# One half of a weight cast from GpSimd to VectorE, and other column groups for the last output tile

## The chip, the cores and the metric

The kernel runs on one core of one Trainium2 chip. Times are device microseconds of whole executions. A profile covers one execution, the span from its first to its last instruction, which is some 1.8 us shorter than the time.

Three marks in the profile are used throughout. H is the start of the first w_in matmul, T the start of the first matmul of the last output tile, and E the end of the span (to a hundredth, from the trace). The span is then the sum of H, the way T - H, and the tail E - T. (Differences are of the rounded marks, so good to 0.01.) The front is the start-up together with the cast of the second weight piece (below), which runs beside the first matmuls.

In the profile's lines PE is TensorE, PEld its weight loads, DVE VectorE, ACT ScalarE, POOL GpSimd and SP SyncE; a q marks an engine's queue, which waits and issues transfers; L385 is a line of the kernel. A timeline's line gives start, length, engine, line, operation, what is written <- what is read, shape and count, and in brackets the idle time before and what ended it.

## The reference

Linear attention, then a feed-forward layer, with the attention's heads side by side as the model dimension:

```python
def _attn_ref(q, k, v):            # 8 batches, 8 heads, 576 rows, 64 columns
    q_s = softmax(q, axis=-1)      # (written out with max, exp, sum)
    k_s = softmax(k, axis=2)       # over the rows
    kv = np.einsum('bhsd,bhse->bhde', k_s, v)
    return np.einsum('bhsd,bhde->bhse', q_s, kv)

def _moe_ref(x, w_in, w_out):      # x 4608 x 512, w_in 512 x 2048, w_out 2048 x 512
    h = x @ w_in
    g = 0.5 * h * (1.0 + erf(h / sqrt(2)))
    return g @ w_out
```

## The kernel before

Inputs and weights come as fp32 and are cast to bf16 on the core. The weights come in pieces, each cast when it has landed; w_in has five, of 256, 256, 512, 512 and 512 columns. The cast of the second is one of the two places that change. (`cast_wi` as it was; `r` is 2 for the second piece, and 4 for the later ones.)

```python
    def cast_wi(i, w, eng):
        n = wi_cols[i]
        r = n // 128
        o = wi_bf[:, :, wi_off[i]:wi_off[i] + n].rearrange("p d (c m) -> p d c m", c=r)
        w = w[:, :, 0:n].rearrange("p d (m c) -> p d c m", c=r)
        if eng == "p":
            for h in range(2):
                nc.gpsimd.tensor_copy(out=o[:, 2 * h:2 * h + 2], in_=w[:, 2 * h:2 * h + 2])
        else:
            for c in range(NDM):
                nc.vector.tensor_copy(out=o[:, c], in_=w[:, c])
    # ...
    for dm in range(NDM):
        cast_wi_dm(0, wi[0], dm, nc.gpsimd)      # first piece, GpSimd, four casts
    # ...
    x_evac(0, 2, "s")                            # xT copies, ScalarE and VectorE
    x_evac(0, 3)
    cast_wi(1, wi[1], "p")                       # second piece, GpSimd, two casts
    table(AF.Gelu)
    # ...
    h_phase(0, {                                 # first w_in matmuls of batch 0
        0: [lambda: cast_wi(2, wi[2], "v")],     # third piece, VectorE, four casts
        # ...
    }, groups={0: 2, 4: 4, 8: 4}, banks={...})
```

`h_phase` begins with column tiles 0 and 1 together (eight matmuls, first piece), then tile 2 and tile 3 (second piece), each over the four contraction blocks `dm`. GpSimd's first cast of the second piece gives blocks 0 and 1, its second gives 2 and 3.

The other place is the end. The last output tile is computed in two column groups, so that most of it is on its way out when the last group finishes:

```python
    def y_last():
        j = J - 1
        for i, (c0, n) in enumerate(((0, 384), (384, 128))):
            ps = psum_y.tile([128, DM], FP32, tag="y")
            for t in range(NDF):
                nc.tensor.matmul(
                    ps[:, 0:n], st[B]["g"][:, t, j * 128:(j + 1) * 128],
                    wo_bf[:, t, c0:c0 + n], start=(t == 0), stop=(t == NDF - 1),
                )
            y_sb = moe_sb.tile([128, DM], FP32, tag="y_sb")
            nc.vector.tensor_copy(out=y_sb[:, 0:n], in_=ps[:, 0:n])
            for b2 in range(2):
                r0 = (2 * j + b2) * S + M
                eng = nc.scalar if b2 else nc.sync
                eng.dma_start(
                    out=out[r0:r0 + R, c0:c0 + n], in_=y_sb[b2 * R:(b2 + 1) * R, 0:n]
                )
```

The softmax here doesn't subtract the row's maximum and nothing guards it: scores larger than these inputs give would overflow.

## Time and profile before

| | before |
|---|---|
| time, median of 3 runs | 279.69 us (279.55 to 280.07) |
| span of the profiled run, E | 277.94 us |
| TensorE busy | 271.6 us, 98% |
| H, T | 14.06, 270.88 us |
| way T - H, tail E - T | 256.82, 7.06 us |

The prediction below shows the page's busy table, the waits and the chain of waits (columns: start, length, what; each piece is what released the next). Only the two copies of the last tile are shown here, by form, from 270 us on. The columns are line, engine, operation, tiles, shape and count, then busy time and mean ns of one, then idle time before.

```profile
L385 DVE COPY y_sb<-ps 128x384 f32<-128x384 f32 x1 | 0.6, 558 | 1.9 <-PE ps L380 1.9
L385 DVE COPY y_sb<-ps 128x128 f32<-128x128 f32 x1 | 0.3, 290 | 0.3 <-PE ps L380 0.3
```

The longer copy has 256 columns more and takes 268 ns more.

### The profile page before, as it was taken

Reading aid. Unit: us, or ns where it says so; the run is one execution under the profiler, and the core shown is the slowest. Engines: PE = TensorE matmul, PEld = TensorE weight load, DVE = VectorE, ACT = ScalarE, POOL = GpSimd, SP = SyncE. Lnnn points to the kernel's source line nnn. Section 1 sums busy time; section 2 is a strip of 40 time slices with the busy share of each in tenths; the row PEclk is TensorE's granted clock in tenths of the full one; section 3 lists DMA queues with packets and bytes.
Section 4 is the critical chain, followed back from the end, with each engine's and each line's share of the span. In section 5 each row is a group of like instructions: output and inputs, shape, how many; then the busy total and the mean of one; then the engine's idle time right before and its main releaser. Section 6 shows DMA issues by size and latency. Waiting matters only on the chain.

```text
span 277.9 us, 4563 instructions
## 1 busy us (share of the span) xinstructions
PE 271.6 (98%) x1918; PEld 126.1 (45%) x1918; DVE 100.6 (36%) x153; ACT 157.9 (57%) x246; POOL 33.4 (12%) x27
## 2 busy tenths in 40 slices
PE   7799999999999999999999999999999999999995
PEld 3444454444444444444444444444444444444443
DVE  2876574319743540093008400651015200130012
ACT  4867675789377816791569246943683363136400
POOL 1530041002020220014000500050005000000000
PEclk9999999999999999999999999999999999999999
DMA  7999999963992148712981199117502500220033
GB/s 249 396 400 429 398 400 407 398 251 100 297 341 60 68 107 255 294 38 87 247 346 41 43 234 389 46 49 189 115 0 75 151 2 0 75 78 0 0 78 77
DMA packets 44981, 50.10 MB, mean 180 GB/s; under 512 B 20385, under 2 KB 29857, under 8 KB 44705
## 3 DMA queue, kind: packets, MB, share of 16 engines
q1 hardware_dynamic: 44560, 49.39, 53.2%
q10 hardware_dynamic: 400, 0.43, 0.6%
q8 instruction: 15, 0.25, 0.4%
q14 instruction: 6, 0.04, 0.1%
HBM read 36.70 MB, written 9.44 MB: 166 GB/s over the span
## 4 chain that ended last, share of the span: by engine, by line
PE 93%; DMA 4%; POOL 1%; ACTq 0%; SPq 0%; issue 0%; DVE 0%
PE ps L355 44%; PE ps L327 43%; DMA w<-in_moe_w_in_dram 2%; DMA touch<-in_moe_w_in_dram 2%; PE kv L199 2%; PE ps L294 1%; PE ps L380 1%; PE pair L327 1%; POOL wi_bf L428 1%; POOL wi_bf L439 1%; PE ps L299 0%; PE tp L255 0%; ACTq L482 0%; PE ps L255 0%; ACTq L101 0%; SPq L103 0%
## 5 line engine op out<-in xcount | busy, mean ns | idle before, releaser
L327 PE MATMUL ps<-xT,wi_bf 128*128 128x512 bf16 x568 | 125.1, 379 | 0.1
L355 PE MATMUL ps<-wo_bf,g 128*128 128x512 bf16 x560 | 124.2, 379 | 0.0
L333 ACT ACTIVATE g<-ps 128x512 bf16<-128x512 f32 x142 | 83.6, 598 | 67.0 <-PE ps L327 66.9
L327 PEld LDWEIGHTS <-wi_bf 128*128 128x128 bf16 x576 | 56.1, 98 | 68.2 <-POOL wi_bf L428 0.5
L355 PEld LDWEIGHTS <-g 128*128 128x128 bf16 x560 | 53.9, 98 | 64.3 <-issue 0.4
L363 DVE COPY y_sb<-ps 128x512 f32<-128x512 f32 x33 | 22.6, 686 | 81.0 <-PE ps L355 80.6
L238 POOL TENSOR_TENSOR e<-e,recq 128x2048 bf16<-128x2048 bf16 (+1 forms) x9 | 25.7, 2856 | 175.3 <-DVE recq L237 147.2
L162 DVE CAST v_aug<-f 128x576 bf16<-128x576 f32 x24 | 16.4, 745 | 48.8 <-DMA f<-in_v_dram 48.8
L236 DVE TENSOR_REDUCE qsum<-e 128x16 f32<-128x1024 bf16 (+1 forms) x13 | 21.1, 1620 | 13.9 <-ACT e L145 13.9
L320 ACT CAST xT<-ps 128x512 bf16<-128x512 f32 x18 | 9.9, 588 | 28.1 <-PE ps L294 18.1
L145 ACT ACTIVATE e<-f 128x512 bf16<-128x512 f32 (+1 forms) x42 | 20.5, 556 | 3.2 <-DMA f<-in_q_dram 3.0
L150 ACT ACTIVATE ek<-f 128x2304 bf16<-128x2304 f32 (+1 forms) x10 | 17.2, 1728 | 0.6 <-DMA f<-in_k_dram 0.6
L318 DVE CAST xT<-ps 128x512 bf16<-128x512 f32 x17 | 11.0, 685 | 17.0 <-PE ps L294 14.1
L79 ACT ACT_TABLE_LOAD x9 | 11.5, 1283 | 2.8 <-issue 2.6
L472 PE MATMUL ps<-zeros 128*128 128x512 f32 x14 | 8.6, 779 | 1.4 <-DVE zeros L497 1.4
L145 ACT ACT_TABLE_LOAD x7 | 9.0, 1283 | 0.1
L431 DVE CAST wi_bf<-w 128x512 bf16<-128x512 f32 x12 | 7.4, 648 | 2.2 <-DMA w<-in_moe_w_in_dram 2.0
L199 PEld LDWEIGHTS <-ek 64*64 64x64 bf16 x576 | 6.4, 105 | 2.7 <-issue 0.6
L199 PE MATMUL kv<-v_aug,ek 64*64 64x65 bf16 x576 | 6.8, 193 | 0.5 <-POOL v_aug L162 0.5
L238 DVE TENSOR_TENSOR e<-e,recq 128x1024 bf16<-128x1024 bf16 x4 | 6.3, 1565 | 0.1
L472 PEld LDWEIGHTS ps<-zeros 128*128 128x128 f32 x14 | 3.5, 258 | 5.7 <-issue 4.3
L294 PE MATMUL ps<-qT,kvc 64*64 64x512 bf16 x62 | 5.4, 389 | 0.4 <-DVE kvc L218 0.4
(37 smaller groups left out, 49.9 us busy)
## 6 DMA issues: line engine op xcount, KB each, us to landing
out_dram<-y_sb SPq DMA_DIRECT2D x32, 256.0 KB, 2.4
f<-in_k_dram SPq DMA_DIRECT2D x6, 1152.0 KB, 10.2
f<-in_v_dram SPq DMA_DIRECT2D x6, 1152.0 KB, 11.8
f<-in_q_dram SPq DMA_DIRECT2D x6, 1024.0 KB, 7.2
w<-in_moe_w_in_dram SPq DMA_DIRECT2D x6, 512.0 KB, 8.6
f<-in_v_dram SPq DMA_DIRECT2D x8, 288.0 KB, 6.6
f<-in_q_dram SPq DMA_DIRECT2D x4, 512.0 KB, 8.8
w<-in_moe_w_out_dram SPq DMA_DIRECT2D x2, 1024.0 KB, 11.6
```

The costliest lines, as they stand in the source:

```text
L79: nc.scalar.activation(out=scr[:, 1:2], in_=scr[:, 0:1], func=func)
L145: nc.scalar.activation(out=dst[:, i], in_=src[:, u], func=AF.Exp)
L150: nc.scalar.activation(out=ek[b % 2][:, i:i + n], in_=st[b]["kf"][:, i:i + n].rearrange("p x (n d) -> p x n d", n=NS), func=AF.Exp,)
L162: eng.tensor_copy(out=o, in_=i)
L199: nc.tensor.matmul(st[b]["kv"][hp][c, 0:D + 1], ek[b % 2][pr, hp, n, :], v_aug[b % 2][pr, hp, n, 0:D + 1], start=(n == 0), stop=(n == NS - 1),
L236: nc.vector.reduce_sum(out=qsum, in_=eq[:, :, hs, :], axis=AX.X)
L238: eng.tensor_tensor(out=eq[:, :, hs, :], in0=eq[:, :, hs, :], in1=recq.unsqueeze(3).to_broadcast([128, J, w, D]), op=ALU.mult,)
L327: nc.tensor.matmul(ps, wi_bf[:, dm, t * 128:(t + 1) * 128], st[c]["xT"][:, dm, :], start=(dm == 0), stop=(dm == NDM - 1),)
L333: nc.scalar.activation(out=st[c]["g"][:, t, :], in_=ps, func=AF.Gelu)
L355: nc.tensor.matmul(ps, st[c]["g"][:, t, j * 128:(j + 1) * 128], wo_bf[:, t, :], start=(t == 0), stop=(t == NDF - 1),)
L363: nc.vector.tensor_copy(out=y_sb, in_=ps)
L472: nc.tensor.matmul(ps, z[:, 0:128], z, start=True, stop=True)
```

## The change

Its intent: the second half of the second piece should be ready sooner, since VectorE is idle beside GpSimd there; and the first group of the last tile should leave sooner.

```diff
-        for i, (c0, n) in enumerate(((0, 384), (384, 128))):
+        for i, (c0, n) in enumerate(((0, 320), (320, 192))):
...
-        if eng == "p":
-            for h in range(2):
-                nc.gpsimd.tensor_copy(out=o[:, 2 * h:2 * h + 2], in_=w[:, 2 * h:2 * h + 2])
+        if eng == "pv":
+
+            nc.gpsimd.tensor_copy(out=o[:, 0:2], in_=w[:, 0:2])
+            nc.vector.tensor_copy(out=o[:, 2:4], in_=w[:, 2:4])
...
-    cast_wi(1, wi[1], "p")
+    cast_wi(1, wi[1], "pv")
```

## The prediction

> **What bounds the kernel now.** I read the page's busy table and its 40 slices first, then TensorE's waits, then the chain of waits in order of time, and last the timelines of the two places that the change touches.
>
> ```profile
> PE 271.6 (98%) x1918; PEld 126.1 (45%) x1918; DVE 100.6 (36%) x153; ACT 157.9 (57%) x246; POOL 33.4 (12%) x27
> ...
> PEclk9999999999999999999999999999999999999999
> ```
>
> TensorE is busy for 271.6 of 277.9 us at the full clock; no other engine reaches 60%. Work moved between GpSimd (12%) and VectorE (36%) is therefore worth only what TensorE waits for it.
>
> ```profile
> PE ps L472 <- DVE zeros L497: 1.4, 1, 1.4
> PE ps L255 <- DVE e L238: 0.5, 1, 0.5
> PE kv L199 <- POOL v_aug L162: 0.5, 1, 0.5
> PE ps L294 <- DVE kvc L218: 0.4, 1, 0.4
> ```
>
> These are all the waits of the matmul row: 2.8 us, all in the first 14 us, and none of them is for the cast that the change splits. That wait shows only in the chain of waits, because the modelled end of the matmul before it covers the gap:
>
> ```profile
> 13.27 0.05 issue
> 13.32 1.48 POOL wi_bf L439 x4
> 14.80 1.59 POOL wi_bf L428 x2
> 16.40 0.05 issue
> 16.45 5.35 PE ps L327 x24
> ...
> 271.04 3.51 PE ps L380 x32
> 274.55 0.02 issue
> 274.57 0.29 DVE y_sb L385
> ```
>
> Between 16.45 and 274.55 us the chain is TensorE alone, back to back. So there are just two places at which this change can act: the moment before 16.45, where the chain arrives from GpSimd's two casts (L428), and the end, after the last matmul. Everything between is passed on unchanged unless a new gap opens.
>
> At the first place the timelines of weight loads, GpSimd and VectorE read:
>
> ```profile
> 14.05 1.84 PEld L327 LDWEIGHTS <-wi_bf 128*128 128x128 bf16 x10 [0.23 <-issue]
> 16.44 0.55 PEld L327 LDWEIGHTS <-wi_bf 128*128 128x128 bf16 x4 [0.55 <-POOL wi_bf L428]
> ...
> 14.75 0.64 POOL L428 CAST wi_bf<-w 128x512 bf16<-128x512 f32 x1
> 15.34 1.05 POOL L428 CAST wi_bf<-w 128x512 bf16<-128x512 f32 x1
> ...
> 13.58 1.32 DVE L318 CAST xT<-ps 128x512 bf16<-128x512 f32 x2
> 15.25 2.15 DVE L431 CAST wi_bf<-w 128x512 bf16<-128x512 f32 x3 [0.36 <-DMA w<-in_moe_w_in_dram]
> 18.53 0.62 DVE L431 CAST wi_bf<-w 128x512 bf16<-128x512 f32 x1 [1.13 <-DMA w<-in_moe_w_in_dram]
> ```
>
> Ten weight loads run before the gap: eight for the first two column tiles (first w_in piece) and two for tile 2, that is, contraction blocks 0 and 1, which GpSimd's first cast wrote. The eleventh needs block 2, from the second cast, and waits. VectorE is empty from the end of its two xT copies (13.58 + 1.32 = 14.90) to 15.25, where it waits for the next piece's transfer.
>
> **What the Trainium skill says.** "SBUF — State Buffer", section "Who interferes with whom": GpSimd and a VectorE copy or cast in a two-port mode lock a shared port pair against each other, and the one that issued first makes the other wait. The trace agrees that they disturb each other, though not with a clean lock: GpSimd's cast took 0.64 us beside VectorE's copies from PSUM and 1.05 us beside the L431 casts, and of those the one that began at 15.89 took 0.97 where the median is 0.62. "TensorE: Matmul & The Clock Gate", section "Back-to-back issue gap", gives N/2.4 + 2.5 ns warm: 216 ns for 512 columns, 162 for 384, 136 for 320, 82.5 for 192, 56 for 128. The trace agrees: 10.36 us for 48 matmuls of 512 columns in the chain is 216 ns, and 16 x (162 + 56) = 3.49 us against the chain's 3.51. "DMA: Bandwidth & Descriptors", section "Specifications", puts the smallest transfer at line rate at 512 B; the last piece's rows of 128 columns already are 512 B, and of 192 columns 768 B, so no threshold is crossed.
>
> **The change, part by part.**
>
> Part one, the cast. Removed: one GpSimd cast of 128x512. Added: one VectorE cast of the same size. The gap is worth less than it looks. Weight loads sat idle 0.55 us, but matmuls had one in hand. The first of the ten starts at 14.06 and they follow at 0.216, so an eleventh without a wait starts at 14.06 + 10 x 0.216 = 16.22. It started at 16.45. Hence at most 0.23 us.
>
> Does the new order free all of it? VectorE is free at 14.90. Unhindered, the new cast takes some 0.62 us (like L431's 128x512 casts) and ends at 15.5. If GpSimd's cast, begun at 14.75, holds it up, add the 0.35 us that L431 lost in such an overlap: 15.9. Block 2 is wanted by a weight load at about 16.0, so even then it is there. GpSimd's remaining cast covers blocks 0 and 1, wanted by the weight load at 15.58: undisturbed it ends at 14.75 + 0.64 = 15.39, in time; if instead it is the one slowed to 1.05 us, it ends at 15.80, and the matmul due at 15.79 starts at about 15.95, which gives back 0.16 us. GpSimd starts 0.15 us ahead, so I hold the first more likely (two in three): 0.23 x 2/3 + 0.07 x 1/3 = 0.18 us gained.
>
> Is it given back behind? VectorE's three casts of the third piece start up to 0.65 us later, from 15.5 to 15.9, but lose the collision that cost 0.35; they end at 17.4 to 17.8, before the fourth waits for its transfer until 18.53. From there VectorE's times stand. TensorE, 0.23 earlier, meets these: block 3 of the third piece, cast by 18.53 + 0.62 = 19.15, wanted at about 20.1; the transfer-bound v casts of batch 1, which GpSimd ends at 42.84, against matmuls that would start at 43.41 - 0.23 = 43.18. Both hold, so the gain goes through to the end. The weight buffer of the second piece is also freed up to 0.5 us sooner, which lets a w_out load be queued earlier, but the DMA slices there read 9 and the rate is some 400 GB/s: it is queued behind others and lands at the same time.
>
> Part two, the last tile. Matmuls: 16 x (136 + 82.5) = 3.50 us against 3.49, no change in the end of TensorE. The two L385 copies took 558 ns (384 columns) and 290 ns (128 columns): 268 ns for 256 columns, 1.05 ns each, so 491 ns for 320 and 357 ns for 192. The last copy lies bare after the last matmul, and so costs 357 - 290 = 0.07 us. The first copy starts 16 x (162 - 136) = 0.42 us earlier and is done before the last one can start, as it is now (273.68 + 0.56 = 274.24 against 274.57); that saves nothing, for the last group's chain doesn't pass through it. The first pieces' transfers are issued earlier too, but they are not last: issued at 274.27 with 2.4 us to land they are home at 276.7, the last ones issued at about 274.9 with 2.0 to 2.1 at 276.9 to 277.0. The last transfers grow from 32 to 48 KB each. The pairs of 96 and 32 KB differ by 0.1 to 0.3 us for 64 KB, so 16 KB more is worth 0.03 to 0.08. Together the tail gets 0.12 us longer.
>
> Sum: -0.18 + 0.12 = -0.06, with the tail certain in sign and the front certain in neither size nor neighbours. 279.69 - 0.06 = 279.6 us.
>
> **The rivals.** (1) VectorE's cast slows GpSimd's, and the wait moves from block 2 to block 0. For it: the 1.05 and 0.97 us above. Against: GpSimd's 0.15 us lead. The front then gains 0.07, the tail costs 0.12: 279.75. (2) TensorE's earlier run meets a transfer-bound wait later and the 0.23 is lost. For it: slices of DMA at 9 up to about 60 us, and the v cast with 0.3 us of slack. Against: both slacks computed above exceed the shift. Then only the tail counts: 279.8. (3) The longer last copy doesn't show, because the completion of the first pieces' writes, earlier by 0.42, clears the queue for the last: then the tail is 0 to +0.05, and the time 279.5. (4) A large effect: it would need TensorE to lose its back-to-back run between 16 and 274 us; nothing in the diff touches that.
>
> **Range and chances.** All rivals lie within 279.45 to 279.85. The three runs of before spread by 0.5 us (279.55 to 280.07), more than those rivals do, and sets the range: 279.2 to 280.0. 2% is 5.6 us, more than all the idle time of TensorE after its warm-up, and no rival comes near it: within 2% at 0.985, faster 0.005, slower 0.01.
>
> **What would show it right or wrong.** Right: the chain of waits passes from the GpSimd cast of the first piece to TensorE without a 0.55 us wait on the second; the first 24 matmuls after the gap start near 16.2; the last two copies read near 491 and 357 ns; the end comes 3.5 us after the last copy begins (now 277.94 - 274.57 = 3.37). Wrong: GpSimd's cast takes over 0.8 us and a weight load waits for it near 15.6 (rival 1); a new wait of TensorE between 18 and 45 us on a cast or transfer (rival 2); the new VectorE cast well off 0.6 to 0.95 us; or the distance from last matmul to the end shrinking rather than growing by about 0.1.

## The result, and the profile after

| | before | after |
|---|---|---|
| time, median of 6 runs | 279.59 us (279.49 to 280.07) | 279.67 us (279.54 to 279.69) |
| span of the profiled run, E | 277.94 | 277.88 |
| H, T | 14.06, 270.88 | 14.20, 270.78 |
| way T - H | 256.82 | 256.58 |
| tail E - T | 7.06 | 7.10 |

The ratio is 1.000, with a 95% interval of 0.9987 to 1.0012: no difference that these runs resolve, and it would take some 0.35 us to be seen.

The chain of waits of the changed kernel, from the first w_in matmul on and at the end:

```profile
13.58 0.58 ACT xT L320
14.16 0.04 issue
14.20 0.81 PE ps L327 x3
15.01 0.05 issue
15.06 6.64 PE ps L327 x30
...
270.94 3.51 PE ps L380 x32
274.45 0.02 issue
274.47 0.36 DVE y_sb L385
```

The chain no longer comes from GpSimd's casts but from ScalarE's copy of the first xT tile. (The piece at 15.01 is a matmul whose record is missing: the trace has 28 matmul records fewer than before's.) The way is 0.24 us shorter, just the gap that the prediction computed. But H itself is 0.14 us later, and the tail 0.04 longer; 0.06 us is left.

The timelines of GpSimd and VectorE there:

```profile
14.54 0.64 POOL L428 CAST wi_bf<-w 128x512 bf16<-128x512 f32 x1
14.81 0.65 DVE L429 CAST wi_bf<-w 128x512 bf16<-128x512 f32 x1
15.56 1.97 DVE L432 CAST wi_bf<-w 128x512 bf16<-128x512 f32 x3
```

Both halves are there by 15.46, before the weight loads want them. And the copies of the last tile:

```profile
L385 DVE COPY y_sb<-ps 128x320 f32<-128x320 f32 x1 | 0.5, 492 | 1.5 <-PE ps L380 1.5
L385 DVE COPY y_sb<-ps 128x192 f32<-128x192 f32 x1 | 0.4, 358 | 0.8 <-PE ps L380 0.8
```

The copies take the 491 and 357 ns that were predicted, within 1 ns.

One reading of this is that a gain of 0.24 us was eaten by a start-up that the change had moved. A second is that the start-up varies anyway. A third is that the gap itself is a chance of one profile. The experiments tell them apart.

### The profile page after: what moved, and what is told of

Same layout as the page of the kernel before. It is cut to its first block, busy times and chain, and to the rows that moved or that the text cites. A ratio compares the mean times of both kernels' runs of the same rounds, so it can differ in the third digit from the quotient of the medians. Undisturbed runs are those within 1.5% of the kernel's fastest.

```text
span 277.9 us, 4535 instructions
## 1 busy us (share of the span) xinstructions
PE 269.7 (97%) x1890; PEld 126.7 (46%) x1918; DVE 101.0 (36%) x154; ACT 157.6 (57%) x246; POOL 32.5 (12%) x26
## 4 chain that ended last, share of the span: by engine, by line
PE 93%; DMA 4%; issue 1%; POOL 0%; ACT 0%; DVE 0%; SPq 0%
PE ps L327 44%; PE ps L355 43%; DMA f<-in_v_dram 2%; PE kv L199 2%; PE ps L294 2%; DMA f<-in_q_dram 2%; PE ps L380 1%; PE pair L327 1%; POOL v_aug L162 0%; PE ps L299 0%; ACT xT L320 0%; PE tp L255 0%; PE ps L255 0%; DVE y_sb L385 0%; SPq L103 0%
## 5 line engine op out<-in xcount | busy, mean ns | idle before, releaser
L355 PE MATMUL ps<-wo_bf,g 128*128 128x512 bf16 x543 | 122.1, 379 | 1.6 <-issue 1.1
L162 DVE CAST v_aug<-f 128x576 bf16<-128x576 f32 x24 | 16.4, 746 | 47.6 <-DMA f<-in_v_dram 47.6
```

The lines of the kernel that those rows point to most:

```text
L162: eng.tensor_copy(out=o, in_=i)
L355: nc.tensor.matmul(ps, st[c]["g"][:, t, j * 128:(j + 1) * 128], wo_bf[:, t, :], start=(t == 0), stop=(t == NDF - 1),)
```

## The experiments

Eleven runs, all with correct results. Where nothing is said of the diff, the rest is the kernel before. Times are medians, set against the kernel before in the same rounds and on the same chip. (e1 to e4 and e9 to e11 ran on one chip, e5 to e8 on another; e5, on the second chip, has the way and the tail of the changed kernel within 0.01 us.) The marks of all thirteen profiles:

| profile | cast | last groups | H | way T - H | tail E - T |
|---|---|---|---|---|---|
| before | GpSimd twice | 384, 128 | 14.06 | 256.82 | 7.06 |
| e1 | GpSimd twice | 384, 128 | 14.31 | 256.58 | 7.02 |
| e10 | GpSimd twice | 384, 128 | 13.98 | 256.63 | 7.02 |
| e3 | GpSimd twice | 320, 192 | 14.04 | 256.87 | 7.10 |
| e9 | GpSimd twice | 256, 256 | 14.21 | 256.57 | 7.24 |
| e6 | GpSimd twice | 128, 384 | 14.19 | 256.59 | 7.61 |
| e7 | GpSimd twice | 448, 64 | 14.16 | 256.59 | 7.68 |
| e4 | GpSimd three times | 384, 128 | 14.12 | 257.27 | 7.06 |
| after | both engines | 320, 192 | 14.20 | 256.58 | 7.10 |
| e2 | both engines | 384, 128 | 14.34 | 256.60 | 7.04 |
| e11 | both engines | 384, 128 | 14.11 | 256.58 | 7.02 |
| e8 | both engines | 384, 128, copy split | 14.10 | 256.58 | 7.30 |
| e5 | VectorE twice | 320, 192 | 14.12 | 256.58 | 7.11 |

### e1: the kernel before against itself

No edit.

> The kernel before, unchanged, timed against itself: the noise of the comparison and a second profile of it. Every theory: ratio 1.000, within 0.1%. If my reading of the first profile is sound, a weight load of the w_in phase again waits about 0.55 us for GpSimd's second cast, and the way from the first w_in matmul to the first matmul of the last tile again takes 256.8 us (in the changed kernel's profile 256.6). If instead the start-up (until the first w_in matmul, 14.06 before and 14.20 after) varies from run to run by 0.1 us or more with nothing changed, then the start-up hid the gain in the changed kernel's profile. Rival: the change itself moved the start-up; then this run starts at 14.06 within 0.05.

Measured: 279.66 us against 279.61, ratio 1.0002 (0.9989 to 1.0014). H is 14.31, and the way is 256.58, as in the changed kernel. The chain of waits of this second profile of the same kernel:

```profile
13.15 1.13 POOL wi_bf L439 x3
14.28 0.03 issue
14.31 7.50 PE ps L327 x34
```

34 matmuls run on without a gap. So my reading that the 0.55 us wait belongs to the kernel fell: there is none here, though GpSimd's second cast was as slow as in the first profile. The timelines of VectorE and GpSimd:

```profile
15.08 0.63 DVE L431 CAST wi_bf<-w 128x512 bf16<-128x512 f32 x1
15.15 1.07 POOL L428 CAST wi_bf<-w 128x512 bf16<-128x512 f32 x1
```

It ended at 15.15 + 1.07 = 16.22. The eleventh matmul, which needs it, is due at H + 10 x 0.216 = 14.31 + 2.16 = 16.47. TensorE was late itself, so nothing waited. And the start-up moved by 0.25 us with nothing changed, more than the 0.14 between before and after.

### e2: the cast alone

The `cast_wi` part of the change, groups 384 and 128.

> Only the cast is split between GpSimd and VectorE; the last tile as before (384 and 128). Theory: the wait of 0.23 us at the second cast is gone and nothing gives it back: 256.6 us from the first w_in matmul to the last tile, last matmul to end as before, time 0.2 us shorter (0.07%). Rival (given back later): the way takes 256.8 us as before, with a new wait between 18 and 45 us, time as before. GpSimd's one cast 0.64 us, VectorE's 0.65 us as in the changed kernel.

Measured: 279.55 us against 279.61, ratio 0.9998 (0.9985 to 1.0010). The way is 256.60 and nothing is given back behind. But the same way stands in e1 without the change, so the 0.2 us is no difference between the kernels as such.

### e3: the last tile alone

```diff
-        for i, (c0, n) in enumerate(((0, 384), (384, 128))):
+        for i, (c0, n) in enumerate(((0, 320), (320, 192))):
```

> Only the last tile's groups are 320 and 192; the cast as before, both halves on GpSimd. Theory: the way from the first w_in matmul to the last tile is 256.8 us as before; from the start of the last copy to the end 3.43 to 3.5 us against 3.37 before, so the time is 0.06 to 0.12 us longer. Rival (the tail costs nothing because the first pieces' transfers are out of the way sooner): 3.37 or less, time as before.

Measured: 279.76 us against 279.61, ratio 1.0002 (0.9990 to 1.0015). The tail is 7.10 and the last copy to the end 3.40 us, just below what the theory gave. The way was a surprise: 256.87, with no wait for GpSimd (its two casts took 1.23 us and ended at 15.81). Here TensorE started early, at 14.04, and the third w_in piece landed late, at 15.8, and the later ones behind it. Two weight loads then waited, from the waits of the weight-load row:

```profile
PEld L327 <- DVE wi_bf L431: 0.7, 2, 0.4
...
PEld L355 <- DVE wo_bf L465: 0.2, 1, 0.2
```

In the chain the first cost TensorE 0.13 us (16 matmuls of the last w_in piece took 3.58 us where before took 3.45). The last w_in cast ended at 25.10, and its matmul was due at about 25.06 (in before's timeline the matmuls of that piece begin at 24.66, the fourth of them, which needs that cast, 0.65 later, which is H + 11.02 once the gap of 0.23 is taken off). The rest of the 0.29 over 256.58 was lost between 38.3 and 39.4, before the matmuls that need the first cast of the last w_out piece, which ended at 39.34. So an early TensorE can be held up by the weights' own stream.

### e4: a wait put in on purpose

```diff
-            for h in range(2):
-                nc.gpsimd.tensor_copy(out=o[:, 2 * h:2 * h + 2], in_=w[:, 2 * h:2 * h + 2])
+            nc.gpsimd.tensor_copy(out=o[:, 0:2], in_=w[:, 0:2])
+            nc.gpsimd.tensor_copy(out=spare, in_=w[:, 0:2])
+            nc.gpsimd.tensor_copy(out=o[:, 2:4], in_=w[:, 2:4])
```

> The kernel before with one more GpSimd cast of 128x512, into a spare tile, between the two halves: the second half is ready later by the length of one more cast, 0.64 to 1.05 us. Theory (a wait at this place goes to the end one to one): the way from the first w_in matmul to the last tile grows by the same 0.64 to 1.05 us over 256.8, time 280.2 to 280.7. Rival (slack behind this place takes it up, so that the 0.23 us taken away bought nothing either): the time grows by less than half of the delay, under 0.35 us.

Measured: 280.05 us against 279.61, ratio 1.0011 (0.9997 to 1.0024). The way is 257.27, that is 0.69 over 256.58. The chain of waits:

```profile
14.73 0.59 POOL wi_bf L428
15.32 0.59 POOL spare L429
15.91 1.00 POOL wi_bf L430
16.91 0.05 issue
16.96 5.35 PE ps L328 x24
```

The eleventh matmul was due at 14.12 + 2.16 = 16.28 and came at 16.96: a wait of 0.68. It went into the way in full. (The forecast had counted a whole cast's length, from 256.8; it is the wait that goes into the way, counted from 256.58, so way and time came out below it.) The time alone, with an interval that reaches 1, would not carry this; the profile does. So a wait here does cost its length, and the question is only how often there is one.

### e5: both halves on VectorE

```diff
-            nc.gpsimd.tensor_copy(out=o[:, 0:2], in_=w[:, 0:2])
+            nc.vector.tensor_copy(out=o[:, 0:2], in_=w[:, 0:2])
             nc.vector.tensor_copy(out=o[:, 2:4], in_=w[:, 2:4])
```

(This is an edit of the changed kernel.)

> The changed kernel with both halves of the second piece cast by VectorE, none by GpSimd, so no GpSimd cast runs beside VectorE's. It measures VectorE's form of this cast alone. If the 0.65 us of the changed kernel was VectorE unhindered, both casts take 0.62 to 0.68 here; if it was a faster cast held up by GpSimd (the port lock that the skill tells of), they take 0.35 to 0.5. Second: the casts of the third piece take 0.62 each, never 0.97, since the collision needs GpSimd. Time: the first half is ready at about 15.5 to 15.6, so TensorE waits 0 to 0.3 us there: 279.6 to 279.9.

Measured: 279.68 us against 279.58, ratio 1.0003 (0.9989 to 1.0017). The timeline of VectorE:

```profile
14.73 0.42 DVE L428 CAST wi_bf<-w 128x512 bf16<-128x512 f32 x1
15.06 0.42 DVE L429 CAST wi_bf<-w 128x512 bf16<-128x512 f32 x1
```

Unhindered, this cast takes 0.42 us, not the 0.62 that I took over from the casts of the later pieces, so in the changed kernel it was held up. In the four profiles with both engines GpSimd kept its 0.64 to 0.65 and VectorE took 0.65, 0.69, 0.79 and 0.88, longer the sooner after GpSimd it began. Each time it ended 0.28 or 0.29 us after GpSimd did (after: 15.18 and 15.46; e11: 15.32 and 15.61). That is the port lock that the prediction cites, with GpSimd, which issued first, holding it. With both casts on VectorE the piece is ready at 15.48, as soon as with both engines: the split as such saves nothing over giving VectorE the whole.

### e6, e7, e9: the last tile in other groups

The tuple in `y_last` becomes ((0, 128), (128, 384)), ((0, 448), (448, 64)) and ((0, 256), (256, 256)).

> The kernel before with the last tile's groups turned round, 128 and then 384 columns: the last copy is the long one. From the first matmul of the last tile to the end it was 7.02 to 7.07 us with a last group of 128, 7.10 with 192. Theory (the tail grows by the copy alone, 1.05 ns a column, and the larger transfers add nothing or take 0.02 away): 7.05 + 0.27 = 7.3. Rival (my prediction's term for the transfers, 0.03 to 0.08 us for each 16 KB): 7.05 + 0.27 + 0.12 to 0.32 = 7.45 to 7.65. Time 279.8 to 280.2. The front is the one before: a stall at the second cast only if the first w_in matmul is early (14.1 or before) and VectorE's casts of the third piece overlap the second GpSimd cast.

Measured: 280.05 us against 279.58, ratio 1.0017 (1.0005 to 1.0030). The tail is 7.61, not 7.3: my theory that it grows by the copy alone fell, and the rival's 7.45 to 7.65 has it. (The last copy began 3.74 us after T instead of 3.69: between the two groups one step from a matmul's start to the next is 107 ns long where its neighbours are 56. So 0.05 of it is TensorE's.) From the start of the last copy to the end it is 3.87 us where a last group of 128 has 3.33 to 3.37. The copy is 0.27 of the 0.52; the other 0.25 comes with transfers of 96 for 32 KB.

> The kernel before with groups of 448 and 64 columns. The last copy should take 223 ns (0.067 less). Theory 1: matmuls of 64 columns run at 64/2.4 + 2.5 = 29 ns apart, the matmuls in all take 3.49 us as now and the tail from the first matmul of the last tile to the end is 6.97. Rival: the weight load of 128 columns paces them at 50 to 60 ns (or more), the matmuls take 0.35 to 0.5 us longer and the tail 7.3 to 7.5. The front as in the kernel before, with the same condition for a stall.

Measured: 280.21 us against 279.58, ratio 1.0023 (1.0010 to 1.0037): the only other clear difference. The tail is 7.68. Theory 1 had the matmuls right and the tail wrong: the 64-column matmuls start 29 ns apart, not paced by their weight loads, and all 32 span 3.66 us in the timeline, as with 384 and 128. The timelines of VectorE and SyncE tell where the time went:

```profile
273.98 0.76 DVE L385 COPY y_sb<-ps 128x448 f32<-128x448 f32 x2 [2.33 <-PE ps L380]
274.63 1.11 SPq L389 DMA_DIRECT2D out_dram<-y_sb  x2
...
275.19 0.55 SPq L389 DMA_DIRECT2D out_dram<-y_sb  x1
```

The last copy stood behind the first, and ended at 274.74; its transfer was issued at 275.19, because the queue was still issuing the first piece's. So the last piece lost 0.4 us in the queue. Its two transfers took another 2.18 and 2.26 us to land although they have 16 KB (1.99 and 2.15 for before's 32 KB), in rows of 256 bytes and right behind 112 KB; which of these two counts, no run tells.

> The kernel before with the last tile in two groups of 256 columns: the point between a last group of 192 (tail 7.10 from the first matmul of the last tile to the end) and 384 (7.61). The last copy should take 424 ns, 0.134 over 128 columns'. If each further 16 KB of a last transfer costs some 0.06 us from 48 KB on (what 384 against 192 says once the copy's 0.20 is taken off: 0.31 for 48 KB is 0.1 for each 16 KB), the tail is 7.10 + 0.067 + 0.06 to 0.1 = 7.23 to 7.27. If the transfers cost nothing up to 64 KB, 7.17. Time 279.7 to 279.9.

Measured: 279.77 us against 279.46, ratio 1.0010 (0.9996 to 1.0024). The tail is 7.24 and the copy 0.42, as expected with a cost for the transfers: from the last copy's end to the end of the span are 3.12 us. Beside it, from the other runs: 3.03 to 3.08 for a last group of 128 columns, 3.05 to 3.06 for 192, 3.31 for 384. Against 32 KB, then, 48 KB add nothing, 64 KB 0.07 and 96 KB 0.25 us. These are net figures: with a wider last group the first piece also leaves sooner, which e8 bears on.

### e8: the last copy on two engines

The cast as changed, groups 384 and 128, and:

```diff
-            nc.vector.tensor_copy(out=y_sb[:, 0:n], in_=ps[:, 0:n])
+            m = n if i == 0 else n // 2
+            nc.vector.tensor_copy(out=y_sb[:, 0:m], in_=ps[:, 0:m])
+            if m < n:
+                nc.scalar.copy(out=y_sb[:, m:n], in_=ps[:, m:n])
```

> The version that the runs so far point to: the cast split as in the change, the last tile's groups 384 and 128 as before, and the last 128-column copy shared by VectorE and ScalarE, 64 columns each. Theory: VectorE's part takes 223 ns; if ScalarE's takes no more than 250, the tail from the first matmul of the last tile to the end is 7.05 - 0.04 to 0.07 = 7.0; no stall at the second cast, so 256.6 us from the first w_in matmul to the last tile. Time 279.5, within 0.1% of both kernels. Rival: the second engine's start or its wait costs as much as the shared columns save; 7.05 or more.

Measured: 279.84 us against 279.58, ratio 1.0008 (0.9995 to 1.0020), and a tail of 7.30, 0.26 over the mean of 7.04. The timelines of VectorE and ScalarE:

```profile
274.07 0.54 ACTq L392 DMA_DIRECT2D out_dram<-y_sb  x1
...
274.37 0.23 DVE L386 COPY y_sb<-ps 128x64 f32<-128x64 f32 x1 [0.34 <-PE ps L380]
274.80 0.21 ACT L388 COPY y_sb<-ps 128x64 f32<-128x64 f32 x1 [13.69 <-DVE y_sb L386]
275.05 0.50 ACTq L392 DMA_DIRECT2D out_dram<-y_sb  x1
```

The second copy began 0.2 us after the first had ended, so nothing was shared in time. The profile puts the wait down to VectorE's copy (ended 274.59), but ScalarE's own queue was issuing the first piece's transfer until 274.61, and the chain of waits passes through that issue. Which of the two held it is not settled; that two writers of one tile are put in order, though their columns are apart, would be one reason. The rival had it: the version that was to beat both is worse.

A by-product: the last transfers, 32 KB each as in the kernel before, were issued here 0.44 us after the first piece's issue on ScalarE was over, not right behind it. ScalarE's issue took 0.50 us (0.74 to 0.75 in the six profiles with 384 and 128 columns and one copy), and from the end of the last copy to the end of the span are 2.97 us, not 3.03 to 3.08.

### e10, e11: a third profile of before, a second of the cast alone

No edit, and the edit of e2.

> A third profile of the unchanged kernel, and a second comparison of it with itself. Account to be tested: the second GpSimd cast ends late (the pair takes 1.6 us) when the third piece has landed by about 15.3, else 1.23 us; TensorE waits there only if that end, plus 0.05, comes after the first w_in matmul plus 2.16; and the way from there to the last tile is 256.58 plus whatever waits the chain shows. In four of five profiles with this front so far there was no wait, so most likely none here; rival: the wait is the rule and those four were chance.

> A second sample of the cast alone. The way from the first w_in matmul to the last tile is 256.58 to 256.60 again, the GpSimd cast 0.64, VectorE's 0.65 to 0.8 (0.42 of its own plus being held up by GpSimd). Against the kernel before the time is the same within the interval; if the wait of 0.23 had been the rule in the kernel before, the two samples of this one would be 0.2 us below it, in both.

Measured: e10 279.52 us against 279.46, ratio 1.0007 (0.9993 to 1.0021); e11 279.56 against 279.46, ratio 1.0003 (0.9990 to 1.0015). e11's way is 256.58. e10's is 256.63, with no wait at GpSimd's cast; 0.05 is lost near 39.2, at the place that held up e3. Neither sample of the cast alone lies 0.2 us below the kernel before (0.06 below and 0.10 above), as it would if the wait were the rule there. One clause of e10's account fell. The third piece had landed by 15.21, and still GpSimd's pair took 1.22 us, not 1.6. The timelines of GpSimd and VectorE in e10:

```profile
15.13 0.64 POOL L428 CAST wi_bf<-w 128x512 bf16<-128x512 f32 x1
...
15.21 1.04 DVE L431 CAST wi_bf<-w 128x512 bf16<-128x512 f32 x1 [0.52 <-DMA w<-in_moe_w_in_dram]
```

Here GpSimd's second cast began 0.08 us before VectorE's and was spared; VectorE's ended 0.48 after it. In before and in e1 VectorE began 0.09 and 0.07 us ahead, kept its 0.62 to 0.63, and GpSimd's ended 0.51 to 0.52 after VectorE's. (In e9 VectorE began 0.02 ahead, while GpSimd's first cast still ran, and GpSimd won. In e6 and e7 GpSimd was ahead and VectorE's cast ended 0.47 us after it.) But for e9, what decides is the order in which the two begin, here by less than 0.1 us. And that follows from when a transfer lands: in all of these profiles VectorE's first cast of the third piece starts 0.02 us after the landing.

## Why the prediction was right, point by point

**What bounds the kernel.** Right. The way is 256.57 to 256.63 us in ten of thirteen profiles, whatever the front and the tail; TensorE runs back to back there, and what the change can do lies outside.

**The gap of 0.23 us.** Its size was right for the profile it was read from, and the split does away with it: none of the four profiles with both engines has it. The step that failed is the silent one before it: "So there are just two places at which this change can act" takes the gap for a feature of the kernel. In seven profiles of kernels with GpSimd's two casts it is there once. It takes two things at once: GpSimd losing the port to VectorE's third-piece cast, so that its second cast ends at 16.2 to 16.4 instead of 0.6 us after it began (before and e1 alone); and a start early enough that TensorE is there first (before: due at 16.22, ready at 16.39 + 0.05; e1: due at 16.47, ready at 16.27). Averaged over the seven the gap is 0.23 / 7 = 0.03 us, an estimate from few profiles, where the prediction put the gain at 0.18.

**Does GpSimd's cast stay undisturbed.** Right, by the prediction's own likelier branch: it took 0.64 to 0.65 us in all four profiles. VectorE's cast was mis-sized: "some 0.62 us" unhindered is 0.42 (e5), and "0.35 us" for being held up was 0.23 to 0.46, depending on how far GpSimd had come. The two errors cancelled: 15.46 in the changed kernel lies just before the predicted 15.5 to 15.9. The prediction's remark that the engines disturb each other "not with a clean lock" was wrong. Ends 0.28 to 0.29, 0.47 to 0.49 and 0.50 to 0.52 us after the other engine's (by which cast waited), each time, are what a clean lock gives; the recorded duration of the one that waits includes its wait.

**Is it given back behind.** Right for the changed kernel: its way, 256.58, is as short as any. The slacks were computed from one profile, though. Where the weights land later than TensorE starts (e3) they are used up, and 0.29 us goes there instead.

**The tail.** The copy was right to a nanosecond or two (0.068 us against 0.07). The term that failed is the transfers' "0.03 to 0.08" for 32 to 48 KB: net it measured zero, 3.05 to 3.06 us from the end of the last copy to the end against 3.03 to 3.08. So the tail grew by 0.06 (7.10 against a mean of 7.04), not 0.12, and the distance named as a sign, 3.5 us from the start of the last copy to the end, came out as 3.41.

Why the net is zero the runs suggest but don't settle. Set against e8's 2.97 us, where 32 KB met a free queue, 48, 64 and 96 KB add 0.08, 0.16 and 0.34 us, some 0.08 for each 16 KB: the upper end of the prediction's term. And 32 KB right behind the first piece, as in the kernel before, cost 0.07 to 0.12 us more than in e8. With 192 columns last (and with 256 and 384) ScalarE's last issue takes 0.49 to 0.50 us as in e8, not 0.74 to 0.75. By this reading the term was about right, and rival 3, which the prediction counted as an alternative to it, was at work beside it: what the larger transfer costs, the queue that is clear sooner gives back. That rests on one profile of a run made for something else, so it is likely and not shown. e7 shows with more force that the queue matters when the first piece comes late.

**The sum.** -0.18 + 0.12 was put in for what the runs make -0.03 + 0.06. Both are far below what the timing resolves, and both sums are near zero. The range, set by the spread of the runs, held for that reason and not because the parts were right: that is luck as far as the front goes. The medians differ by +0.08 us where -0.06 was forecast, and the sign of the difference is not settled. H varied from 13.98 to 14.34 with nothing before it changed, so the start-up's variation is several times either part. The second reading of the result above is thus borne out, and the third too; that the change moved the start-up is not supported.

No version beat both kernels. The cast alone came out at 279.55 and 279.56 us against 279.61 and 279.46.

## What to carry to other kernels

A wait of a few tenths of a microsecond in the start-up, read from one profile, may be a chance of when the transfers landed: take a second profile of the unchanged kernel before you count on removing it. Compare stages between marks (first matmul to last tile, last tile to end) when the whole time can't resolve a change. When two engines share a port, look at which begins first, and give work to the one that wouldn't wait; at the end of a kernel, weigh the last group's copy, its bytes and the queue in front of it together.

## What the Trainium skill lacked or had wrong

- "SBUF — State Buffer", "Who interferes with whom": the lock and its rule that the first to issue wins agree with the runs (but for e9, where VectorE began 0.02 us ahead and waited). The page lacks how it looks in a trace: the waiting instruction is recorded from its start, so a 0.42 us VectorE cast reads 0.65 to 0.88 and ends 0.28 to 0.29 us after GpSimd's; a 0.64 us GpSimd cast reads 1.05 to 1.07 and ends 0.51 to 0.52 after VectorE's. A lead of 0.06 us was enough (e7, e11).
- "VectorE: DVE Perf Modes", the tier table: it gives 2x to an fp32 copy between places in SBUF. A cast of 512 elements a partition took 0.42 us with source elements 8 bytes apart (e5), which fits (the table has 1227 ns for 2048 elements), but 0.62 with elements 16 bytes apart, with no GpSimd work beside it (e3). The table has no figure for such a step. (The skill does speak of large steps elsewhere, without a figure for such a cast; and no run here changed the step alone.) The slower form still takes and waits for the port.
- "TensorE: Matmul & The Clock Gate", "Back-to-back issue gap": its sustained 131 ns for 512 columns and 81 ns for 128 in streams of weight load and matmul are not seen. Such a stream ran here at 216 ns (48 in 10.36 us), and 16 matmuls of 384 with 16 of 128 columns took 3.51 us, which fits the page's formula for the isolated matmul, 162 and 56 ns.
- Beyond a general fit of a transfer's time to its bytes, on no page that I read: what the size of the last stores costs at the end of a kernel when they are issued from SyncE and ScalarE. For two stores of 32, 48, 64 and 96 KB each, the time from the end of the last copy to the end of the span was 3.03 to 3.08 (2.97 in e8), 3.05 to 3.06, 3.12 and 3.31 us.
